# A transformer block on one core: token tile 5 turned on TensorE, values made by head group, loads paced, and odd tiles normalized on GpSimd

## The chip, the cores and the metric

The kernel runs on one core of a Trainium2 chip. A core has five engines, each with its own stream of instructions in a fixed order: TensorE (PE; its weight loads are shown as PEld), VectorE (DVE), ScalarE (ACT), GpSimd (POOL) and SyncE (SP), which here only starts transfers. Sixteen DMA engines move data between HBM and the on-chip memory (SBUF). TensorE writes its results into PSUM, eight banks of 512 fp32 per partition. The metric is device time in microseconds (us) of one execution, as a median over runs.

## The reference, cut to what matters

```python
def _layernorm(x, axis=-1, eps=1e-5):
    m = jnp.mean(x, axis=axis, keepdims=True)
    v = jnp.var(x, axis=axis, keepdims=True)
    return (x - m) / jnp.sqrt(v + eps)

def _A_ref(x, wqkv, wo):          # x: 1 x 2048 x 1024, wqkv: 1024 x 3072, wo: 1024 x 1024
    H = 32; Dh = 32
    qkv = (x @ wqkv).reshape(B, S, 3, H, Dh).transpose(2, 0, 3, 1, 4)
    q, k, v = qkv[0], qkv[1], qkv[2]
    scores = jnp.einsum("bhqd,bhkd->bhqk", q, k) * (Dh ** -0.5)
    p = _softmax(scores, axis=-1)
    o = jnp.einsum("bhqk,bhkd->bhqd", p, v)
    return o.transpose(0, 2, 1, 3).reshape(B, S, D) @ wo

def _B_ref(x, w1, b1, w2, b2):    # w1: 1024 x 3584, w2: 3584 x 1024
    y = _layernorm(x, axis=-1)
    h = _gelu(jnp.einsum("bsd,df->bsf", y, w1) + b1)
    return jnp.einsum("bsf,fd->bsd", h, w2) + b2

xn = _layernorm(x, axis=-1)
out = x + _A_ref(xn, wqkv, wo) * _silu(_B_ref(xn, w1, b1, w2, b2))
```

All inputs are bf16. Every token row of `x` is normalized; the normalized rows feed 32-head attention without a mask and, normalized once more, an MLP. The attention's output is multiplied by the silu of the MLP's output and added to `x`.

## The kernel before, in words

**Tiling.** The 2048 tokens are 16 tiles of 128, the 32 heads 8 head groups of four heads (128 columns of Q, of K and of V). A head group is worked in 8 blocks of 256 queries, a block in 8 units of 256 keys. One unit is 8 score matmuls (L846) into two pairs of PSUM banks and, for each pair, one exponential on ACT over 128 x 1024 scores (L855), which writes a buffer `P`. There are 8 x 8 x 8 units, thus 1024 exponentials. The products P x V (L612) and the sums of the exponentials follow them: DVE adds the buffers up in a tree (L872 and L886, for the first blocks `tree1`, L1209), or PE sums them with a column of ones. All dense work is put between the scores on PE: the projections to Q, K and V of the next head group (`proj`), the MLP, and the product with `wo` at the end. Silu, gelu and most PSUM evacuations are on ACT and DVE.

**Order.** No loop of the kernel issues instructions. Each helper (`dma`, `pool`, `dve`, `act`, `chunk`) adds an operation with its assumed length, a priority and its tokens read and written to `_Plan`. Dense PE work is gathered into items (`_Item`), each a list of matmuls into one PSUM bank with the evacuation behind it, and stands in named queues ("tr", "pro", "q0", "v0", "proj", "mlp", "w2", "wo" among them) with a position, a due time and a `hold`, both counted in score groups. `_Plan.run` plays all engines in assumed time: score matmuls go first on PE, then P x V and the dense items (`pe_step`); the other engines take the ready operation of the lowest priority number (`pick`). What comes out is one fixed order for every engine, and `settle` and `emit` put the semaphore waits into it. A changed length or priority thus moves the order around it too. At run time each engine goes through its order and stands at a wait until it is met; SP is a single queue through which all loads, DMA transposes and stores are started one after the other.

**The start, which the change touches.** Tile t of `x` is loaded into a buffer `xst` (`load_x`, L626). There are ten, all in the memory that is `hT` later; tiles 0 to 9 are issued at the head of SP's queue, with the first head group's weights of K and Q (`load_qk`, `wqk`) behind tile 3, and the weights of V for two head groups (`load_v`, `wv`, 512 KB) behind tile 9. Tiles 10 to 15 reuse buffers, so each of their loads waits for an earlier normalize (`load_x(t, [first[2 * n - 5]])`). For every tile, or for pairs of tiles from tile 4 on:

- DVE takes the statistics with two `bn_stats` (L785), a `bn_aggr` (L788) and an add of eps (L792). Tile 1 is the exception: ACT takes its sums in two passes over 128 x 1024 (`AT = 1`).
- GpSimd raises variance plus eps to the power -0.5 (L794).
- DVE normalizes (`normalize`, L748) into one of four buffers `xnb`, which lie in the memory that is `gw` later.
- Tiles 0 to 3 are turned on PE by eight transposes into one PSUM bank each (`tr_item`) and copied to `xnT` by ACT (L737). Tiles 4 to 15 are turned by DMA transposes that SP starts (L752).

From the turned tiles PE makes Q and K of the first head group in pairs of tiles: `q_item` for the pairs 0 to 2, larger Q pieces behind them, and `k_item` for all eight pairs n = 0 to 7. DVE casts Q to bf16 (L712, L702), ACT casts K (L722). The first scores need pair 0; each further pair of K opens another eighth of the keys. The first three query blocks are worked in an interleaved order while the tiles still come in, and their `P` lie partly in memory that belongs to `w1r`, `w2r`, `V`, `QKT` and `hT` later. V of the first two head groups is made together by eight `v_item`s (16 matmuls of 256 columns each, then one evacuation on DVE, L690) that are held back to the score groups 6 to 13.

When all tiles have been normalized, five GpSimd instructions on 128 x 16 (L818 to L822) work out the factors of the second layernorm, and the MLP can begin.

Of the kernel before, what the change touches and what calls it, by code (L numbers as in the profile page):

```python
# [6 lines left out]
ACT = mybir.ActivationFunctionType  # L7
# [25 lines left out]
class _Plan:  # L33
# [59 lines left out]
    def run(self):  # L93
# [152 lines left out]
        def pe_step(t):  # L246
# [69 lines left out]
            elif v_ok and (mode in "rv" or not d_ok or S["s"] == len(self.s_queue)):  # L316
                use = "v"
            elif d_ok:
                use = "d"
            if use is None:  # L320
# [140 lines left out]
def bass_recurrent_scan__mha_block__mixer_channel_mlp__prompt_kernel(  # L461
# [31 lines left out]
    with ExitStack() as st:  # L493
# [7 lines left out]
        NTR, NWARM, NG0, AT = 4, 8, 3, 1  # L501
# [44 lines left out]
        xst = [h_flat[:, i * 1024:(i + 1) * 1024] for i in range(NXS)]  # L546
        xnb = [gw[:, i * 1024:(i + 1) * 1024] for i in range(4)]
# [72 lines left out]
        XS = lambda t: ("xst", t % NXS)  # L620
# [4 lines left out]
        def load_x(t, extra=()):  # L625
            dma(f"x{t}", lambda e: e.dma_start(xst[t % NXS], x2[t * 128:(t + 1) * 128, :]), 262144, [], [XS(t)],  # L626
# [11 lines left out]
        def load_v(pr):  # L638
            src = A_wqkv[:, 2 * D + pr * 256: 2 * D + (pr + 1) * 256].rearrange("(c p) n -> p c n", p=128)
            dma("wv", lambda e: e.dma_start(wv[:], src), 524288, [], [("wv",)], prio=2, rate=200.0)  # L640
# [5 lines left out]
        for t in range(4, NXS):  # L646
            load_x(t)
        load_v(0)
# [44 lines left out]

        def qk_item(hg, which, tq, wi, pos):
# [21 lines left out]
        def k_item(n):  # L716
            it = _Item("pro", 0.01 * n)
            for dc in range(DC):
                def fn(e, b, dc=dc):
                    return mm(e, bank(b, 0, 256), wqk[wk0][:, dc, :], xnT[:, dc, n * 256:(n + 1) * 256], dc == 0, dc == DC - 1)  # L720
                chunk(it, fn, Q256, [("xnT", 2 * n, dc), ("xnT", 2 * n + 1, dc), ("wqk", wk0)])
# [3 lines left out]

        def tr_item(t):
            it = _Item("pro", t - 10.0)
            it.bank = [2, 3, 4, 5][t]
            tk = ("S", it.bank // 2, it.bank % 2)
# [17 lines left out]
        def normalize(t, rs):  # L747
            first[t] = dve(lambda e: e.tensor_scalar(xnb[t % 4], xst[t % NXS], mv[:, t, 0:1], lnp[:, t, 1:2],  # L748
                                          op0=ALU.subtract, op1=ALU.mult), c_b4(1024) + 118,
                [XS(t), ("mv", t), rs], [("xnb", t % 4)], 1)  # L750
            if t >= NTR:
                dma(f"tr{t}", lambda e: e.dma_start_transpose(xnT[:, :, t * 128:(t + 1) * 128], xnb[t % 4]), 262144,  # L752
                    [("xnb", t % 4)], [("xnT", t, c) for c in range(DC)], prio=0, rate=300.0, occ=1300, lat=1000)
# [10 lines left out]
        for n in range(NPR):  # L764
            groups = [(2 * n,), (2 * n + 1,)] if n < 2 else [(2 * n, 2 * n + 1)]
            for ts in groups:
                if ts == (AT,):
# [698 lines left out]
```

## Time and profile before

The median of three runs is 1036.16 us (1034.75 to 1036.66). One execution was profiled:

| what | value |
|---|---|
| profiled execution, its time | 1036.81 us |
| its span, first to last instruction | 1035.0 us |
| mean granted TensorE clock | 0.997 of full |
| PE busy | 994.5 us, 96% |
| PE weight loads busy | 633.3 us, 61% |
| DVE busy | 955.7 us, 92% |
| ACT busy | 1015.9 us, 98% |
| GpSimd busy | 12.2 us, 1%, 21 instructions |
| ACT's exponentials of 128 x 1024, L855 | 988 of them, 923.6 us |
| DMA moved | 168 MB, 162 GB/s over the span |
| chain that ended last, by engine | ACT 84%, PE 9%, DMA 3%, DVE 2% |

How to read the lines that follow: busy times are sums over instructions, "x24" is a count, and a bracket such as [0.51 <-PE ps L846] says that the engine had stood idle for 0.51 us and that an instruction of line 846 on PE ended this. In a timeline a row begins with the time from the span's start and the length; instructions of one kind that follow each other without a gap share a row with a count, and the length is then that of the whole group. Neighbouring rows can overlap by some 0.1 us: an instruction's row may begin before the row ahead of it has ended. Line numbers are those of the kernel before, and in the profile of the changed kernel those of that kernel, where the same statements stand up to 65 lines lower. The figure behind a DMA group is the median time from issue to landing.

### The profile page before, as it was taken

The numbers are of one execution on the slowest core, as the hardware profiler recorded it, in microseconds if no ns is written. First come the engines' busy times: TensorE is split into PE (matmuls) and PEld (weight loads), VectorE is DVE, ScalarE is ACT, GpSimd is POOL, SyncE is SP. The second block draws the span as 40 slices with busy tenths as digits, with TensorE's granted clock in tenths as the row PEclk, the third lists the DMA queues.
The fourth block names the chain that finished last, engine by engine and source line by source line (L and its number), as shares of the span: only waits on it lengthen the run. The fifth ranks groups of instructions, "written<-read, shape, count | busy, mean of one in ns | idle before, by whom it ended". The sixth has DMA issues, their size and how long they took to land.

```text
span 1035.0 us, 31625 instructions
## 1 busy us (share of the span) xinstructions
PE 994.5 (96%) x14148; PEld 633.3 (61%) x14217; DVE 955.7 (92%) x1343; ACT 1015.9 (98%) x1093; POOL 12.2 (1%) x21
## 2 busy tenths in 40 slices
PE   8999999999999999999999999999999999999996
PEld 6656566666766566666665666666656665654433
DVE  7899999899799999997899999998999889978896
ACT  7999999999999999999999999999999999999996
POOL 2200000000000000000000000000000000000000
PEclk9999999999999999999999999999999999999998
DMA  7967756545766657446457575565365762963321
GB/s 204 171 155 212 192 151 188 166 114 153 205 182 143 177 163 221 120 133 190 136 147 196 149 224 164 149 181 160 84 165 161 208 177 70 294 209 121 121 84 53
DMA packets 318199, 167.99 MB, mean 162 GB/s; under 512 B 56688, under 2 KB 306032, under 8 KB 318064
## 3 DMA queue, kind: packets, MB, share of 16 engines
q1 hardware_dynamic: 318064, 165.98, 58.1%
q8 instruction: 111, 1.82, 0.7%
q14 instruction: 24, 0.20, 0.1%
HBM read 146.55 MB, written 12.06 MB: 153 GB/s over the span
## 4 chain that ended last, share of the span: by engine, by line
ACT 84%; PE 9%; DMA 3%; DVE 2%; issue 0%; SPq 0%; POOL 0%; DVEq 0%; another core or an unknown queue 0%
ACT P L855 78%; PE ps L617 6%; ACT ut L1040 4%; DMA w2r<-in_B_w_dram 2%; PE ps L846 2%; PE ps L612 1%; ACT gw L1067 1%; ACT P L1157 1%; DVE stats L785 1%; DMA xnT<-gw 0%; DMA hT<-in_A_x_dram 0%; DVE gw L748 0%; DVE PA L872 0%; DVE hT L1391 0%; ACT w2r L855 0%
## 5 line engine op out<-in xcount | busy, mean ns | idle before, releaser
L855 ACT ACTIVATE P<-ps 128x1024 bf16<-128x1024 f32 x988 | 923.6, 1238 | 2.9 <-PE ps L846 2.8
L872 DVE TENSOR_TENSOR PA<-P 128x2048 bf16<-128x2048 bf16 x173 | 209.5, 1215 | 33.5 <-ACT P L855 32.4
L617 PE MATMUL ps<-yT,w1r 128*128 128x256 bf16 x1792 | 228.2, 273 | 0.8 <-DVE QKT L702 0.5
L617 PE MATMUL ps<-w2r,hT 128*128 128x256 bf16 x1792 | 223.7, 273 | 4.0 <-DMA w2r<-in_B_w_dram 2.6
L846 PE MATMUL ps<-QKT 32*128 32x256 bf16 x4032 | 200.2, 273 | 12.9 <-ACT P L855 9.3
L886 DVE TENSOR_TENSOR PR<-PR,PA 128x2048 bf16<-128x2048 bf16 x173 | 209.4, 1211 | 1.3
L617 PEld LDWEIGHTS ps<-yT,w1r 128*128 128x128 bf16 x1792 | 163.6, 98 | 54.8 <-issue 30.2
L617 PEld LDWEIGHTS ps<-w2r,hT 128*128 128x128 bf16 x1792 | 163.3, 98 | 54.6 <-issue 30.8
L846 PEld LDWEIGHTS ps<-QKT 32*128 32x128 bf16 x4032 | 59.8, 92 | 142.1 <-ACT P L855 135.3
L612 PE MATMUL ps<-P,V 128*32 128x256 bf16 (+1 forms) x4080 | 136.8, 272 | 0.3 <-issue 0.3
L617 PE MATMUL ps<-xnT,wqk 128*128 128x512 bf16 (+1 forms) x507 | 118.7, 360 | 7.2 <-issue 2.0
L612 PEld LDWEIGHTS ps<-P,V 128*32 128x32 bf16 x4080 | 95.8, 96 | 31.3 <-issue 22.5
L617 PE MATMUL ps<-wv,xnT 128*128 128x256 bf16 (+1 forms) x575 | 85.8, 285 | 0.9 <-DVE QKT L702 0.7
L617 PEld LDWEIGHTS ps<-xnT,wqk 128*128 128x128 bf16 x560 | 49.3, 98 | 53.7 <-issue 15.6
L1023 DVE TENSOR_TENSOR hT<-ps,b1T 128x512 bf16<-128x512 f32 x112 | 76.4, 682 | 1.8 <-PE ps L617 1.1
L872 DVE TENSOR_TENSOR PR<-P 128x2048 bf16<-128x2048 bf16 x60 | 72.6, 1210 | 1.0 <-ACT P L855 0.8
L617 PEld LDWEIGHTS ps<-wv,xnT 128*128 128x128 bf16 x576 | 53.0, 98 | 22.2 <-issue 9.3
L1040 ACT ACTIVATE ut<-ut 128x2048 bf16<-128x2048 bf16 (+1 forms) x33 | 62.1, 1883 | 0.0
L941 DVE STREAM_TRANSPOSE nt<-ps 128x256 f32<-128x256 f32 x63 | 27.8, 442 | 14.9 <-PE ps L612 14.8
L702 DVE CAST QKT<-ps 128x512 bf16<-128x512 f32 x58 | 39.6, 683 | 1.8 <-PE ps L617 1.4
L1037 DVE TENSOR_TENSOR ut<-hT 128x2048 bf16<-128x2048 bf16 (+1 forms) x33 | 34.7, 1052 | 0.1
L1042 DVE TENSOR_TENSOR hT<-ut,hT 128x2048 bf16<-128x2048 bf16 (+1 forms) x33 | 34.6, 1050 | 0.0
(107 smaller groups left out, 581.3 us busy)
## 6 DMA issues: line engine op xcount, KB each, us to landing
w1r<-in_B_w_dram SPq DMA_DIRECT2D x112, 512.0 KB, 4.5
w2r<-in_B_w_dram SPq DMA_DIRECT2D x128, 448.0 KB, 4.6
hT<-in_A_x_dram SPq DMA_DIRECT2D x20, 256.0 KB, 3.8
wqk<-in_A_wqkv_dram SPq DMA_DIRECT2D x16, 256.0 KB, 4.3
yst<-in_A_x_dram SPq DMA_DIRECT2D x16, 256.0 KB, 4.7
g_scratch<-gw SPq DMA_DIRECT2D x32, 128.0 KB, 3.8
o_scratch<-ot SPq DMA_DIRECT2D x56, 64.0 KB, 3.6
xnT<-o_scratch SPq DMA_DIRECT2D x7, 512.0 KB, 7.2
```

The source lines that it names most:

```text
L612: ins = e.matmul(dst(j), lhsT=lhsT(j), rhs=rhs(j), start=start, stop=stop, tile_position=(0, 32 * j), skip_group_check=True)
L617: return e.matmul(dst, lhsT=lhsT, rhs=rhs, start=start, stop=stop, skip_group_check=True)
L702: dve(lambda e: e.tensor_copy(QKT[sl][:, which, tq * 512:(tq + 1) * 512], bank(it.bank)), c_ps(512), [], [(nm, sl, 2 * tq), (nm, sl, 2 * t ...
L846: ins = e.matmul(bank(b0[j], kk * 256, (kk + 1) * 256), lhsT=QKT[sl][32 * j:32 * j + 32, 1, kb * 128:(kb + 1) * 128], rhs=QKT[sl][32 * j:3 ...
L855: x = act(lambda e, h=h: e.activation(Pt[pi][:, 2 * h:2 * h + 2].rearrange("p j k q -> p (j k q)"), ps[:, pr[h] * 1024:(pr[h] + 1) * 1024] ...
L872: return dve(lambda e: e.tensor_tensor(dst[:].rearrange("p u j q -> p (u j) q"), src[:].rearrange("p u j k q -> p (u j) k q")[:, :, 0, :], ...
L886: return dve(lambda e: e.tensor_tensor(fl3(pr), fl3(pr), fl3(PA[i]), op=ALU.add), c_b16(2048), [("PA", i), tok], [tok], 3.2)
L941: dve(lambda e: e.transpose(nt_t[:], bank(pv.bank, 256, 512)), c_ps(256) + 120, [], [("nt",)], prio, pv)
L1023: w1_ev[p] = dve(lambda e: e.tensor_tensor(hT[:, hs], bank(it.bank).rearrange("p (k t) -> p k t", k=2), b1T[:, 2 * pi:2 * pi + 2].unsqueez ...
L1037: dve(lambda e: e.tensor_tensor(u_, x_, x_, op=ALU.mult), c_b16(n), hs_, [("ut", ui)], gp)
L1040: act(lambda e: e.activation(u_, u_, ACT.Tanh, scale=GC), c_acts(n), [("ut", ui)], [("ut", ui)], ga)
L1042: dve(lambda e: e.tensor_tensor(x_, u_, x_, op=ALU.mult), c_b16(n), [("ut", ui)] + hs_, hs_, gp)
```

## The change

The change is made in the start of the kernel and in what feeds it; the rest of the program text is the same, though the planner writes its whole order anew.

1. **Tile 5 on PE** (`TRP = (5,)`). It is turned by PE and copied by ACT like tiles 0 to 3, without a DMA transpose. Its item stands in the queue "pro" just ahead of K of its pair, and `pe_step` lets an item of the queue "tr" in between two matmuls of another item.
2. **Statistics of tile 3 on ACT**, in two passes as for tile 1 (`AT = (1, 3)`).
3. **GpSimd normalizes tiles 7, 9, 11, 13 and 15** (`PN`); DVE keeps the others. The planner assumes 2000 ns for one.
4. **K casts.** For the pairs n = 3 to 7 DVE casts K; ACT keeps n = 0, 1 and 2.
5. **First Q and K in 128 columns.** `qk_first` takes the place of `q_item(0)` and `k_item(0)`: Q and K of tile 0, then those of tile 1 by halves, in 128-column matmuls. K of the pair 1 is split by tile too.
6. **Loads.** There are 16 buffers for tiles of `x`: six more, in the memory of `PR` and `yst`. Tiles 0 to 11 are loaded up front; tiles 12 and 13, the weights of V, and tiles 14 and 15 wait for the normalize of tile 4 (`first[4]`). The loads of the second head group's K weights wait for the normalize of tile 15 instead of tile 9.
7. **V by head group.** `v_half` makes V of one head group for four tiles (32 matmuls of 128 columns, one evacuation). Four of them, for head group 0, stay in the start, held to the score groups 6, 8, 10 and 12; the four of head group 1 become items of the projections that run during head group 0, at the positions 8, 18, 28 and 38.
8. **Smaller ones.** The priority of `tree1` is 2.3 instead of 3.2; the assumed latencies of the DMA transposes of tiles 4, 6 and 7 are longer.

In instructions, the planned PE stream has 14,355 matmuls instead of 14,217, ACT's 1088 activations instead of 1090, DVE's 28 `bn_stats` instead of 30 and 163 tensor copies instead of 158; SP starts 27 DMA transposes instead of 28.

```diff
+            tq, th = self.dense["tr"], heads["tr"]
+            if use is None and S["do"] is not None and th < len(tq) and tq[th].chunks[0].left == 0 and tq[th].chunks[0].ready <= t:
+                heads["tr"] += 1
+                tq[th].k = 1
+                S["mode"] = "d"
+                commit(tq[th].chunks[0], t)
+                return
...
-        NTR, NWARM, NG0, AT = 4, 8, 3, 1
+        TRP = (5,)
+        PN = (7, 9, 11, 13, 15)
+        NTR, NWARM, NG0, AT = 4, 8, 3, (1, 3)
...
+            xst += [pr_flat[:, 0:1024], pr_flat[:, 1024:2048]]
+        xst += [yst_t[i][:] for i in range(2)]
...
-        for t in range(4, NXS):
+        for t in range(NTR, 12):
             load_x(t)
-        load_v(0)
...
+        def v_half(h, m, kind, pos=0.0):
+            it = _Item(kind, pos)
+            for t4 in range(4):
+                for dc in range(DC):
+                    def fn(e, b, t4=t4, dc=dc):
+                        tb = 4 * m + t4
+                        return mm(e, bank(b, t4 * 128, (t4 + 1) * 128), xnT[:, dc, tb * 128:tb * 128 + 128],
+                                  wv[:, dc, h * 128:(h + 1) * 128], dc == 0 and t4 == 0, dc == DC - 1)
+                    chunk(it, fn, Q128, [("xnT", 4 * m + t4, dc), ("wv",)])
+            a = V_SLOTS[0][h]
+            dve(lambda e: e.tensor_copy(V[:, a, 4 * m:4 * m + 4, :], bank(it.bank).rearrange("p (t n) -> p t n", t=4)),
+                c_ps(512), [], [("V", a, 2 * m), ("V", a, 2 * m + 1)], 0, it)
+            return it
...
+            for lo, w in ((0, 128), (128, 128)) if n < 2 else ((0, 256),):
...
+            if n >= 3:
+                dve(lambda e: e.tensor_copy(QKT[0][:, 1, n * 256:(n + 1) * 256], bank(it.bank, 0, 256)), c_ps(256), [],
+                    [("K", 0, n)], -1, it)
+                return it
             act(lambda e: e.activation(QKT[0][:, 1, n * 256:(n + 1) * 256], bank(it.bank, 0, 256), ACT.Copy), c_act(256), [],
                 [("K", 0, n)], -1, it)
...
+        def qk_first():
+            it = _Item("pro", -0.001)
+            for lo, d0, d1 in ((0, 0, 8), (128, 0, 4), (128, 4, 8)):
+                for k, wi in ((0, wq0), (1, wk0)):
+                    for dc in range(d0, d1):
...
+            act(lambda e: e.activation(QKT[0][:, 1, 0:256], bank(1, 0, 256), ACT.Copy), c_act(256), [("S", 0, 1)], [("K", 0, 0)], -1)
+            return it
...
+            rw = ([XS(t), ("mv", t), rs], [("xnb", t % 4)], 1)
+            first[t] = pool(nf, 2000, *rw) if t in PN else dve(nf, c_b4(1024) + 118, *rw)
+            if t >= NTR and t not in TRP:
                 dma(f"tr{t}", lambda e: e.dma_start_transpose(xnT[:, :, t * 128:(t + 1) * 128], xnb[t % 4]), 262144,
...
+            if n == 6:
+                for t in range(12, NT):
+                    load_x(t, [first[4]])
+                    if t == 13:
+                        load_v(0, [first[4]])
...
-                    if t >= NXS:
-                        load_x(t, [first[2 * n - 5]])
...
+            pro_q += [tr_item(t) for t in (2 * n, 2 * n + 1) if t in TRP]
...
-        for n in range(NPR):
-            plan.dense["v0"].append(v_item(0, n, "pro", 0.2 + 0.01 * n))
-            plan.dense["v0"][-1].hold = 6 + 1 * n
+        for n in range(NPR // 2):
+            plan.dense["v0"].append(v_half(0, n, "pro", 0.2 + 0.01 * n))
+            plan.dense["v0"][-1].hold = 6 + 2 * n
...
-            wk = load_qk(hg, 1, [first[9]] if hg == 1 else ())
+            wk = load_qk(hg, 1, [first[NT - 1]] if hg == 1 else ())
...
+            if hg == 1:
+                lst += [(8 + 10 * n, "v1", n) for n in range(NPR // 2)]
```

## The prediction

> **What bounds the kernel now.** I read the busy shares by stretch first, because a mean over the whole span mixes the start with the rest. Columns: busy time (instructions) of PE, PEld, DVE, ACT, POOL, then the granted clock, the DMA share and GB/s.
>
> ```profile
> 0.00:20.00 20.00, 17.34 (x241) 14.95 (x241) 16.11 (x43) 13.69 (x19) 4.40 (x12) 1.00 0.76 213
> 20.00:40.00 20.00, 16.95 (x195) 11.53 (x188) 16.22 (x39) 18.25 (x24) 2.62 (x5) 1.00 0.92 209
> 40.00:60.00 20.00, 18.88 (x360) 13.07 (x359) 18.65 (x31) 19.69 (x24) 5.16 (x6) 1.00 0.95 163
> ...
> 200.00:300.00 100.00, 99.53 (x1414) 66.50 (x1416) 90.90 (x118) 100.00 (x108) 0.00 (x0) 1.00 0.59 161
> ```
>
> From 60 us to 1025 us ACT is the bound: 100.00 of 100 us, and the clock is 1.00, so no throttle is in it. What the change does before 60 us therefore reaches the end one for one, as a shift of ACT's queue, and nothing else counts unless PE, DVE or DMA fall behind ACT later. Second, ACT's own order of time from the first exponential on (start, length, what; in brackets its idle time):
>
> ```profile
> 12.73 1.02 ACT L855 ACTIVATE P<-ps 128x1024 bf16<-128x1024 f32 x1 [0.51 <-PE ps L846]
> 13.65 1.02 ACT L737 ACTIVATE xnT<-ps 128x1024 bf16<-128x1024 bf16 x1
> ...
> 16.70 4.69 ACT L855 ACTIVATE P<-ps 128x1024 bf16<-128x1024 f32 x5 [0.51 <-PE ps L846]
> 22.68 0.38 ACT L722 ACTIVATE QKT<-ps 128x256 bf16<-128x256 f32 x1 [1.28 <-PE ps L617]
> 22.96 4.69 ACT L855 ACTIVATE P<-ps 128x1024 bf16<-128x1024 f32 x5
> ...
> 37.83 1.02 ACT L855 ACTIVATE P<-ps 128x1024 bf16<-128x1024 f32 x1 [0.47 <-PE ps L846]
> ...
> 55.74 1.03 ACT L855 ACTIVATE P<-ps 128x1024 bf16<-128x1024 f32 x1
> ```
>
> Five exponentials take 4.69, so one costs (4.69 - 1.02) / 4 = 0.917. A K cast costs 22.96 - 22.68 = 0.28, and 0.26 at other places: 0.27. Between 12.73 and 55.74 stand 40 exponentials, one transpose copy and seven K casts: 36.7 + 0.9 + 1.9 = 39.5 of 43.0 us. **ACT waits 3.5 us there**, longest before the K cast of tiles 4 and 5. Third, the DMA view of 17 to 21.6 us shows why (engines' busy tenths, then queues, then issue to landing):
>
> ```profile
> DMA  8999999940019999999980097203224755899999
> ...
> q8 instruction: 1, 0.02, 1.4%
> ...
> hT<-in_A_x_dram SPq DMA_DIRECT2D x2, 256.0 KB, 3.7
> xnT<-gw SPq DMA_TRANSPOSE x3, 2.9
> ```
>
> The transpose of tile 5 was issued at 17.09 and released PE at 21.55, after 4.46; the usual one takes 2.9. Beside it ran one instruction fetch, and the engines stood still in the middle. Two more transposes took 6.0 in the stretch 29.8 to 37, again beside one fetch. Fourth, GpSimd, because it gets new work:
>
> ```profile
> 7.96 0.78 POOL L794 TENSOR_TENSOR lnp<-lnp,mhalf 128x1 f32<-128x1 f32 x1 [0.56 <-DVE lnp L792]
> ...
> 40.98 0.23 POOL L818 TENSOR_TENSOR lnp<-lnp 128x16 f32<-128x16 f32 x1
> 41.29 0.29 POOL L819 TENSOR_SCALAR lnp<-lnp 128x16 f32<-128x16 f32 x1
> 41.66 3.04 POOL L820 TENSOR_TENSOR lnp<-lnp,mhalf 128x16 f32<-128x16 f32 x1
> 44.78 0.78 POOL L822 TENSOR_TENSOR lnp<-lnp 128x16 f32<-128x16 f32 x1
> ```
>
> L822 is a multiply of the same size as L818 and took 0.78 against 0.23, while DVE ran two-input adds (L1209); L794 took 0.78 at 7.96, beside a DVE normalize, against 0.55 at 6.85. So a GpSimd instruction waits for some DVE ones. The other way round: inside L820 (41.66 to 44.70) DVE's normalizes took 0.99 for two and its adds 0.68 each, as elsewhere. DVE did not wait.
>
> **The change part by part**, summed on ACT's queue.
>
> *First exponential, +0.5.* Tile 3's statistics move from DVE to ACT (two passes, 1.06 each), and the changed order puts the first of them ahead of the copy of tile 0's transpose. x3 is issued at 2.11 and takes 4.9 to land: 7.0. Then 1.05 of pass, and the copy starts at 8.1 instead of 7.31. Copies of tiles 0, 1, 2 (0.92 each) and the second pass (1.05) end at 11.9; the K cast of tiles 0 and 1 follows, and now tile 3's copy (0.92, from 12.3, when PE has turned it) stands before the first exponential, no longer behind it: 13.25. If x3 takes the median 3.8, PE still sets 12.3: the lower end is +0.5 too; with x3 a microsecond later it is +1.5.
>
> *ACT's work, -1.35.* Five of the seven K casts (tiles 6 to 15) go to DVE: 5 x 0.27. Tile 3's copy leaves the stretch, tile 5's enters it (PE turns it now): even. Left: 36.7 + 0.9 + 0.5 = 38.1.
>
> *ACT's waits, 3.5 to 0.6.* K of tiles 4 and 5 needs the DMA only for tile 4 now: normalize at 14.4, issue 15.0, landing 17.9 (2.9). Q and K of that pair are 16 matmuls of 0.11 and follow two score groups: the cast runs at its turn, about 21.8, without a wait. One hole stays behind it, cast to score matmul to exponential, 0.5 as in the rows above. For the later pairs I walked the changed order with the rows' lengths. The five pows come at 19.1, 21.7, 25.8, 28.7 and 33.1, the transposes land in pairs at 24.2 and 25.5, 26.8 and 28.1, 31.5 and 32.8, 34.2 and 35.5, 37.2 and 39.4. Score groups are 1.83 apart and PE is in order, so a late landing holds the scores queued behind it; spare there is 1.3 us for tiles 4, 6, 7, over 2 for 8 and 9, 0.9 for 10 to 13, 0.3 for 14 and none for 15. Undisturbed, this is -2.9. But the same view has one such fetch in each of 17 to 21.6, 29.8 to 37 and 41.9 to 47.3 us, with transposes of 4.5, 6.0 and 4.3 beside it, 1.4 to 3.1 over the usual. The last six transposes are now in flight from 28 to 39 almost without a break, so I expect one to be hit: +1.0. Two hits: +3.1 (1.7 late each, with the queue behind them). None: 0.
>
> *GpSimd normalize, five of them.* The trace has no such row. From below: IOTA 128x128 took 0.24, MEMSET 128x1 0.10, so about 1.1 ns an element, 1.2 us for 1024, and 0.2 fixed: 1.4. From above: L818's 16 elements in 0.23, 8 ns each, 8 us. I take 1.4, nearest to the row with most elements. In the walk the price is free up to 2.2 us, since each one has the gap to the next pow; 2.6 costs 0.8, 3.0 costs 2.0, 3.5 costs 4.1. [...]
>
> *DVE.* It loses five normalizes (0.45 each), two statistics of 0.6 and an aggregate (1.4), gains five K casts (0.34 each): less work, nothing on the path. The eight V evacuations become four (0.61 each) before 40 us.
>
> *PE.* V of the second head group (64 matmuls of 256 columns, 0.11 each, 7 us) leaves the start and comes back as 128 of 128 columns (eight transposes take 0.45, 0.056 each: 7.2 us) up to unit 78. It lies beside PE's 18.9 of 20 us at 60 to 80 and 19.9 at 80 to 100, under an ACT that is always full; cover gone, it would cost up to 7 there, but ACT showed 100.00 with PE at 99.53. Taken: 0.
>
> *SP.* x10 and x11 are issued before any transpose; x12, x13, V's weights, x14, x15 pass behind tile 4's transpose, 1.5 MB that have landed by 23 at some 350 GB/s, the rate of the loads at 12 to 14 us, just ahead of tile 6's. At worst they hold tile 6's landing by 1.0, inside its spare. The second group's K weights wait for the last normalize: needed at 44, landed by 41.
>
> *Tail.* The chain of waits has 1.21 us of "issue" on PE at 1025.82, in the last rush of small matmuls. The instruction count changes by some 270, so it may vanish (-1.2), stay or grow (+1.2); I take 0.
>
> Sum: +0.5 - 1.35 - 2.9 + 1.0 = **-2.75**. The profiled execution took 1036.81 (span 1035.0 and 1.8 around it): 1034.06. The median of the runs is 0.65 lower, so I forecast 1036.16 - 2.75 = **1033.4**. Its own range is 1032.1 to 1034.1.
>
> **Rivals.** *A, slower: DVE waits for GpSimd.* Both normalizes of a pair are released by the same pow, and if GpSimd's comes first DVE stands for its length, five times, with statistics and casts queued behind; DVE is busy 16.2 of 20 us there, so it does not catch up. Walked so, the last pow moves from 33.1 to 36.1 at 1.4 us each, and the loss is 3.0; at 2.0 us it is 5.5. It turns into a loss from 1.4 us on: 1036.4 there, **1038.9** at 2.0. For it: L822 and L794 show that the two do block each other. Against it: DVE ran through L820 unhindered. The Trainium skill, "SBUF — State Buffer", section "Who interferes with whom", states just this: the shared port pair is an exclusive lock, and whichever of the two starts first fully blocks the other for its whole instruction. By that rule L820 should have held DVE until 44.70; this trace disagrees, though L820 reads only 16 elements.
> *B, no change: two landings late.* 1033.4 + 2.1 = **1035.5**. For it: three of twelve transposes were late before.
> *C, slower: GpSimd's price is 3.5 or more* without any lock: 1033.4 + 4.1 = **1037.5**. For it: only rows of 128 elements and fewer exist.
>
> **How the numbers follow.** The smallest change that these runs tell from none is about 0.2%, 2.07 us. Forecast 0.50, B 0.22, A 0.22, C 0.06. Forecast is faster, B the same, A and C slower: 0.50, 0.22, 0.28. The range goes from 1031.5 (no landing late, and most of the tail's hole gone) to 1039.0 (A at 2.0 us); outside are a longer GpSimd normalize with the lock and a double luck, together under 0.2.
>
> **What would show it.** Right: first exponential at about 13.2; ACT's waits under 2 us between it and the exponential after the six into w2r, and that one at about 52 to 53; two K casts left on ACT there; GpSimd normalizes under 2.2 with DVE's normalizes still near 0.54 and no idle time in front of them. Wrong: DVE idle before its normalizes for as long as GpSimd's run (A); transposes of 10 to 15 taking 4 us or more to land, with scores waiting (B); GpSimd's busy time over 15 us (C); or ACT under 99% busy between 60 and 1000 us, which none of my terms has.

## The result, and the profile after

The changed kernel takes 1038.82 us (median, 1036.30 to 1041.04) where the kernel before takes 1036.33 beside it: 1.0024 times as long, 95% interval 1.0015 to 1.0032. It was forecast to be 2.75 us faster and is 2.5 us slower. One execution was profiled, at 1037.8 us with a span of 1036.0, thus a microsecond under its median.

The busy shares by stretch of the changed kernel, with the columns as before (PE, PEld, DVE, ACT, POOL, granted clock, DMA share, GB/s):

```profile
0.00:20.00 20.00, 16.63 (x244) 14.26 (x245) 15.05 (x44) 16.44 (x24) 4.79 (x12) 1.00 0.75 219
20.00:40.00 20.00, 15.20 (x204) 11.42 (x200) 15.24 (x35) 15.42 (x18) 19.47 (x10) 0.91 0.75 159
40.00:60.00 20.00, 16.95 (x284) 10.75 (x286) 14.01 (x23) 16.95 (x19) 8.29 (x6) 0.91 0.65 125
200.00:300.00 100.00, 99.21 (x1380) 65.29 (x1379) 93.78 (x122) 100.00 (x108) 0.00 (x0) 1.00 0.57 155
```

Up to 20 us ACT has more work done than before (16.44 against 13.69). From 20 to 60 us it has 5.6 us less. GpSimd is busy for 19.47 of 20 us, and the granted clock, 1.00 in the same stretches of the kernel before, is 0.91 in two of them. ACT's order of time:

```profile
13.56 1.02 ACT L911 ACTIVATE P<-ps 128x1024 bf16<-128x1024 f32 x1
...
22.97 3.77 ACT L911 ACTIVATE P<-ps 128x1024 bf16<-128x1024 f32 x4 [0.51 <-PE ps L902]
...
31.56 3.77 ACT L911 ACTIVATE P<-ps 128x1024 bf16<-128x1024 f32 x4 [0.82 <-PE ps L902]
38.36 1.94 ACT L911 ACTIVATE hT<-ps 128x1024 bf16<-128x1024 f32 x2 [3.03 <-PE ps L902]
...
48.68 1.94 ACT L911 ACTIVATE w1r<-ps 128x1024 bf16<-128x1024 f32 x2 [2.58 <-PE ps L902]
...
60.03 15.71 ACT L911 ACTIVATE P<-ps 128x1024 bf16<-128x1024 f32 x17
```

The exponential after the six into w2r, the 41st, comes at 60.03 in place of 55.74: 4.3 us later than in the kernel before, where 52 to 53 was forecast. All waits between the first exponential and this one sum to 7.6 us. Part of the loss comes back later: the waits of 0.71 and 0.64 us that the kernel before has at 176.5 and 917.6 us are not there, and the last of the 1024 exponentials is 2.5 us late. In the tail ACT's wait before its last copy is 2.76 us in place of 4.58, and the span ends 1.0 us late (1036.0 for 1035.0).

GpSimd's order of time has the instruction that the prediction could not see (start, length):

```profile
20.12 3.79 POOL L796 TENSOR_SCALAR gw<-hT,mv,lnp 128x1024 bf16<-128x1024 bf16 x1
23.88 0.72 POOL L846 TENSOR_TENSOR lnp<-lnp,mhalf 128x2 f32<-128x2 f32 x1
24.70 4.05 POOL L796 TENSOR_SCALAR gw<-hT,mv,lnp 128x1024 bf16<-128x1024 bf16 x1
28.73 0.71 POOL L846 TENSOR_TENSOR lnp<-lnp,mhalf 128x2 f32<-128x2 f32 x1
29.54 3.78 POOL L796 TENSOR_SCALAR gw<-PR,mv,lnp 128x1024 bf16<-128x1024 bf16 x1
33.29 0.72 POOL L846 TENSOR_TENSOR lnp<-lnp,mhalf 128x2 f32<-128x2 f32 x1
```

A normalize takes 3.78 to 4.05 us, not 1.4. The pow of the next pair (L846) stands behind it without a gap, so GpSimd goes round in 4.6 to 4.9 us. DVE, in order too, waits for that pow (the view of DVE's waits from 19 to 45 us: total, times, longest):

```profile
DVE gw L796 <- POOL lnp L846: 4.7, 3, 1.8
```

Behind DVE's waiting normalize stand its V evacuations (L716). PE's next V item needs the bank that such an evacuation frees; the scores stand behind the item, and ACT waits for the scores. That is the chain into the 3.03 us. It has one more link, in the clock (the busy shares again, microsecond by microsecond):

```profile
33.00:34.00 1.00, 0.21 (x8) 0.00 (x0) 0.00 (x0) 1.00 (x2) 1.00 (x2) 1.00 0.59 127
34.00:35.00 1.00, 0.00 (x0) 0.00 (x0) 0.96 (x3) 1.00 (x2) 0.90 (x2) 1.00 0.52 120
35.00:36.00 1.00, 0.69 (x10) 0.69 (x11) 1.00 (x3) 0.33 (x1) 1.00 (x1) 0.84 0.71 158
36.00:37.00 1.00, 1.00 (x12) 1.00 (x10) 0.97 (x3) 0.00 (x0) 1.00 (x1) 0.50 1.10 247
```

PE stood nearly still for two microseconds (0.21 us of matmuls from 33 to 35), and then, with its work at hand and ACT idle, it ran at half its clock.

### The profile page after: what moved, and what is told of

It reads as the page before. It is cut to its first block, busy times and chain, and to the rows that moved or that the text cites. A ratio compares the mean times of both kernels' runs of the same rounds, so it can differ in the third digit from the quotient of the medians.

```text
span 1036.0 us, 31979 instructions
## 1 busy us (share of the span) xinstructions
PE 1005.2 (97%) x14355; PEld 638.1 (62%) x14355; DVE 955.5 (92%) x1342; ACT 1017.0 (98%) x1093; POOL 32.6 (3%) x26
## 4 chain that ended last, share of the span: by engine, by line
ACT 90%; PE 4%; DVE 2%; POOL 2%; issue 1%; DMA 1%; SPq 0%; DVEq 0%
ACT P L911 82%; ACT ut L1101 4%; PE ps L630 3%; POOL gw L796 1%; ACT gw L1128 1%; ACT P L1221 1%; PE ps L625 1%; DVE stats L837 1%; PE ps L902 1%; ACT w2r L911 1%; POOL lnp L846 0%; DMA hT<-in_A_x_dram 0%; ACT w1r L911 0%; DMA xnT<-gw 0%; DVE gw L796 0%
## 5 line engine op out<-in xcount | busy, mean ns | idle before, releaser
L630 PE MATMUL ps<-xnT,wqk 128*128 128x512 bf16 (+2 forms) x584 | 131.5, 356 | 1.7 <-DMA xnT<-gw 0.6
L630 PE MATMUL ps<-wv,xnT 128*128 128x256 bf16 (+2 forms) x704 | 90.3, 268 | 6.2 <-DVE V L716 3.0
L630 PEld LDWEIGHTS ps<-wv,xnT 128*128 128x128 bf16 x704 | 56.8, 100 | 30.3 <-issue 11.4
```

The lines of the kernel that those rows point to most:

```text
L630: return e.matmul(dst, lhsT=lhsT, rhs=rhs, start=start, stop=stop, skip_group_check=True)
```

## The experiments

The runs are compared by the ratio of their time to that of the kernel before, measured beside them (its medians there were 1035.5 to 1036.3):

| kernel | median us | ratio to before, 95% |
|---|---|---|
| changed | 1038.82 | 1.0024 (1.0015 to 1.0032) |
| before_gp | 1042.23 | 1.0057 (1.0045 to 1.0068) |
| gp512 | 1037.15 | 1.0010 (1.0000 to 1.0019) |
| gp256 | 1036.67 | 1.0003 (0.9995 to 1.0012) |
| gp256_late_yx | 1033.05 | 0.9973 (0.9962 to 0.9983) |
| all_dve | 1032.38 | 0.9966 (0.9954 to 0.9978) |
| all_dve_k_act | 1034.66 | 0.9983 (0.9972 to 0.9995) |
| all_dve_x_late | 1034.48 | 0.9990 (0.9980 to 0.9999) |
| all_dve_v_pairs | 1033.55 | 0.9982 (0.9973 to 0.9990) |
| all_dve_tr5_dma | 1039.80 | 1.0035 (1.0023 to 1.0047) |
| all_dve_wv_late | 1030.95 | 0.9950 (0.9937 to 0.9962) |
| plan_3900 | 1036.42 | 1.0006 (0.9998 to 1.0015) |

The first theory was *price*: the GpSimd normalize is too long. Its rivals were *order* (something else in the new order costs the time) and *lock* (GpSimd and DVE hold each other up, and the row is long only for that).

### Only the GpSimd instruction shorter: gp256 and gp512

```diff
+            w_ = 256 if t in PN else 1024
             def nf(e):
-                return e.tensor_scalar(xnb[t % 4], xst[t], mv[:, t, 0:1], lnp[:, t, 1:2], op0=ALU.subtract, op1=ALU.mult)
+                return e.tensor_scalar(xnb[t % 4][:, 0:w_], xst[t][:, 0:w_], mv[:, t, 0:1], lnp[:, t, 1:2],
+                                       op0=ALU.subtract, op1=ALU.mult)
```

The planner's assumed length stays, so all engines keep the changed kernel's order. In gp512, w_ is 512. The other columns of these five tiles are left out.

> The changed kernel in its own order, but GpSimd normalizes only the first 256 of the 1024 columns of tiles 7, 9, 11, 13 and 15; the other columns of these tiles are left out (they keep an earlier tile's values). Theory price: in the changed kernel such an instruction took 3.79 to 4.05 us and the next pair's pow stood behind it, so that GpSimd went 4.8 us a pair; with a quarter of the columns it takes about 1.1 us, DVE no longer stands before its normalizes (1.27 to 1.77 us each now), and the exponential after the six into w2r comes at 52 to 53 us in place of 60.0; the time is 1032.5 to 1035. Theory order (the new order, the V halves or the paced loads cost the time, not the instruction): GpSimd's rows shrink, but that exponential stays at 57 us or later and the time at 1037 or more.

> As the run with 256 columns, with 512 of 1024 columns normalized by GpSimd and the others left out. Theory price: about 2.0 to 2.1 us an instruction, which the prediction put just under the free limit of 2.2, so within 1 us of the run with 256 columns and 3 to 5 us ahead of the changed kernel. If the loss grows in step with the length instead, it lies a third of the way from the 256-column run to the changed kernel. Theory order: no difference to the changed kernel, 1038 to 1039.

The normalize took 1.22 to 1.49 us with 256 columns and 2.08 to 2.35 with 512. The times are 1036.67 and 1037.15: 2.1 and 1.4 thousandths under the changed kernel, and 0.5 us from each other. So the length counts. That it costs nothing up to some 2.3 us, as the prediction's walk had it (free up to 2.2), shows in the pows of the later pairs: they come at 25.75, 29.89 and 34.20 in gp256 and at 25.71, 29.98 and 34.26 in gp512. The equal totals would not show it alone, since both kernels were then held at one later place, by tile 15's transpose. But neither kernel came down to 1033.4. ACT's order of time in gp256 shows that place:

```profile
34.81 1.95 ACT L913 ACTIVATE hT<-ps 128x1024 bf16<-128x1024 f32 x2
36.62 3.81 ACT L913 ACTIVATE P<-ps 128x1024 bf16<-128x1024 f32 x4
40.23 2.03 ACT L913 ACTIVATE hT<-ps 128x1024 bf16<-128x1024 f32 x2
45.58 1.94 ACT L913 ACTIVATE w1r<-ps 128x1024 bf16<-128x1024 f32 x2 [3.31 <-PE ps L904]
```

Up to the 25th exponential (38.43 in gp256, 39.91 in the kernel before) it was 1.5 us ahead of the kernel before. Then ACT waited 3.31 us at one place, for scores that stood behind the transpose of the last tile. SP's order of time there:

```profile
35.52 1.23 SPq L802 DMA_TRANSPOSE xnT<-gw  x1
36.80 0.58 SPq L1068 DMA_DIRECT2D yst<-in_A_x_dram  x1
37.42 1.24 SPq L802 DMA_TRANSPOSE xnT<-gw  x1
```

The transpose of tile 14 took 2.7 us to land. That of tile 15, issued at 37.42, took 5.4: it landed at 42.83, 1.56 us behind the load into yst (41.27) that went out just ahead of it. In the kernel before, both loads into yst went out at 34.19 and 35.73, ahead of tile 12's transpose. Two edits of the change move them: its x tiles 14 and 15 now lie in the buffers yst, and the loads' own condition, which was tile 11's normalize, is taken out:

```diff
-                    [("yst", t2)], rate=390.0, extra=[first[11]] if c == 0 else [w1_ev[4]] if c == 1 else ())
+                    [("yst", t2)], rate=390.0, extra=[w1_ev[4]] if c == 1 else ())
```

So the first of these loads waits for tile 14's normalize to free its buffer, and falls between the last two transposes. *Order* was right too, at a place of its own.

### The two loads into yst behind the last transpose: gp256_late_yx

```diff
-                    [("yst", t2)], rate=390.0, extra=[w1_ev[4]] if c == 1 else ())
+                    [("yst", t2)], rate=390.0, extra=[first[NT - 1]] if c == 0 else [w1_ev[4]] if c == 1 else ())
```

> The run with 256 columns on GpSimd (the other columns left out), and the first two loads into yst wait for tile 15's normalize, as they are then issued behind its transpose. In the 256-column run that transpose was issued at 37.42, right behind one of these loads, and landed at 42.83, 1.56 us after the load; ACT waited 3.31 us for it. Theory load ahead (a transpose lands only after the loads issued before it): the transpose takes 2.7 to 3.2 us, that wait is under 1 us, the exponential after the six into w2r comes near 53.5 in place of 56.90, and the time is 1032.5 to 1034.5, as the prediction had it for a short GpSimd instruction. Theory instruction fetch (what made it late ran beside it): it stays at 4.5 us or more and the time at 1036 to 1037.

1033.05 us, and the 41st exponential came at 53.99, as *load ahead* had it. But tile 15's transpose still took 4.5 us to land, as *instruction fetch* had it: a fetch ran from 39.07 to 40.1 beside it, and one from 39.16 to 40.3 in gp256. The load's part was about 1 us (5.4 to 4.5). The transpose landed 1.5 us earlier (41.35), the clock, halved in gp256 from 42.75 on, stayed at 1.00, and the wait shrank to 0.71:

```profile
42.94 5.74 ACT L913 ACTIVATE w1r<-ps 128x1024 bf16<-128x1024 f32 x6 [0.71 <-PE ps L904]
48.56 5.61 ACT L913 ACTIVATE w2r<-ps 128x1024 bf16<-128x1024 f32 x6
53.99 13.02 ACT L913 ACTIVATE P<-ps 128x1024 bf16<-128x1024 f32 x14
```

With a GpSimd normalize of the predicted length and this load out of the way, the change gives 1033.05 where 1033.4 was forecast. ACT's waits up to the 41st exponential come to 1.8 us there, for 0.6 and 1.0 in the sum.

### The change without its GpSimd part, and the GpSimd part alone: all_dve and before_gp

```diff
-        PN = (7, 9, 11, 13, 15)
+        PN = ()
```

> The change without its GpSimd part: DVE normalizes all tiles, everything else as in the changed kernel (the planner's order shifts a little around it). Theory price: DVE pays 5 x 0.45 us more, which fits into its idle time between 20 and 45 us; 1033 to 1035.5, ahead of both kernels. Theory order: 1037 or more, as the other parts cost the time.

In before_gp the kernel before gets the other half:

```diff
-            first[t] = dve(lambda e: e.tensor_scalar(xnb[t % 4], xst[t % NXS], mv[:, t, 0:1], lnp[:, t, 1:2],
-                                          op0=ALU.subtract, op1=ALU.mult), c_b4(1024) + 118,
-                [XS(t), ("mv", t), rs], [("xnb", t % 4)], 1)
+            def nf(e):
+                return e.tensor_scalar(xnb[t % 4], xst[t % NXS], mv[:, t, 0:1], lnp[:, t, 1:2], op0=ALU.subtract, op1=ALU.mult)
+            rw = ([XS(t), ("mv", t), rs], [("xnb", t % 4)], 1)
+            first[t] = pool(nf, 2000, *rw) if t in (7, 9, 11, 13, 15) else dve(nf, c_b4(1024) + 118, *rw)
```

> The kernel before with one part of the change alone: GpSimd normalizes tiles 7, 9, 11, 13 and 15. Theory price: about 3.9 us each, the pows of the pairs 8 to 11 and the last normalize come 2 to 4 us later than before; slower than before by 2 to 4.5 us, 1038.5 to 1041. Theory order: the instruction alone does no harm, 1035.5 to 1037.5. Theory lock (GpSimd and DVE hold each other up, by DVE's share of work): DVE's rows beside a GpSimd normalize are longer by about a microsecond each.

all_dve takes 1032.38 us, 0.34% under the kernel before; before_gp takes 1042.23, 0.57% over it and more than expected. One part of the change costs about 6 us in either kernel, and the others together gain 3.5. In before_gp's trace the clock stays at 1.00 until the tail (0.50 only from 1034.94 on), and yet ACT's waits up to the 41st exponential come to 6.9 us. So GpSimd's round can cost this much without the clock.

In all_dve the two last tiles are normalized in one go, and both transposes go out ahead of the yst loads. One large wait is left in its start:

```profile
22.44 3.77 ACT L911 ACTIVATE P<-ps 128x1024 bf16<-128x1024 f32 x4 [0.50 <-PE ps L902]
27.88 1.94 ACT L911 ACTIVATE V<-ps 128x1024 bf16<-128x1024 f32 x2 [1.66 <-PE ps L902]
```

PE had waited for V's weights there (landed at 24.44), and its V matmuls then ran at a granted clock of 0.50 from 24.58 to 28.0: 25 of them took 2.79 us, where the same 25 take 1.57 at 1.00 in all_dve_x_late below. Tile 6's transpose, at 26.74, came late as well. But in the traces of all_dve_k_act and all_dve_v_pairs it lands as late (26.76 and 26.77) while the clock stays at 1.00, and ACT waits only 0.41 and 0.86 us there. So half or more of the 1.66 goes with the halved clock, and this execution (1033.48) was the longest of all_dve's five.

### The GpSimd normalize by itself: price

A small kernel repeats one instruction of each kind, three in a row:

```diff
+            (lambda e: pn(e, 1024), None),
+            (p_small, None),
+            (None, d_alone),
+            (lambda e: pn(e, 1024), d_stats),
+            (lambda e: pn(e, 1024), d_norm),
+            (lambda e: pn(e, 1024), d_add),
+            (lambda e: pn(e, 1024), d_cast),
+            (p_mul, None),
+            (p_copy, None),
```

> A small kernel that computes nothing of the reference (it copies x to the output) and runs the GpSimd normalize by itself: 128 x 1024, 512, 256 and 128 columns with DVE idle, then 128 x 1024 beside a stream of DVE statistics, of DVE normalizes, of DVE two-input adds and of DVE casts from PSUM, and a one-operation multiply and a plain copy. Theory price: about 3.8 us for 1024 columns with DVE idle, 3.4 ns an element (from 1.22, 2.08 and 3.79 us for 256, 512 and 1024 columns in the runs so far), and at most 0.3 us more beside any DVE stream. Theory lock: about 1.4 us alone, and 3 us or more only beside DVE streams; or DVE instructions that stand for the length of a GpSimd one.

GpSimd's order of time. The first four rows are normalizes of 1024 columns beside DVE statistics, DVE normalizes, DVE adds and DVE casts; then the multiply alone and the copy:

```profile
32.76 11.31 POOL L31 TENSOR_SCALAR po<-xa,sc 128x1024 bf16<-128x1024 bf16 x3 [8.00 <-DVE do L74]
45.94 11.90 POOL L31 TENSOR_SCALAR po<-xa,sc 128x1024 bf16<-128x1024 bf16 x3 [1.87 <-DVE ds L55]
63.69 15.42 POOL L31 TENSOR_SCALAR po<-xa,sc 128x1024 bf16<-128x1024 bf16 x3 [5.85 <-DVE do L31]
79.57 11.31 POOL L31 TENSOR_SCALAR po<-xa,sc 128x1024 bf16<-128x1024 bf16 x3 [0.46 <-DVE do L60]
90.98 8.49 POOL L40 TENSOR_SCALAR po<-xa,sc 128x1024 bf16<-128x1024 bf16 x3
99.54 3.00 POOL L45 COPY po<-xa 128x1024 bf16<-128x1024 bf16 x3
```

A normalize takes 3.77 us (11.31 / 3) beside statistics and casts, and 2.08, 1.22 and 0.80 for 512, 256 and 128 columns with DVE idle: some 0.4 us and 3.3 ns an element a partition. With one operation in place of two it takes 2.83, a copy 1.00. So *price* holds for what the kernel does, and *lock* as the cause falls. A part of it is there: beside DVE normalizes it takes 3.97, and DVE's go at about 0.75 each for 0.48 alone (16 in 12.0 us against 4 in 1.92); beside two-input adds it takes 5.14, outside what *price* had expected.

The Trainium skill, "GPSIMD Engine Reference", section 3.1, gives 1.03 cycles an element for bodies of up to two operations and calls about 1.8, at 1.2 GHz, the best case of a tight loop; an estimate from these two figures is 0.9 to 1.5 us for 1024 elements. That is far below the measured 3.77, and the measurement decides. The Trainium skill's advice in the same section, to use DVE for elementwise work, is what these runs come to. By the Trainium skill, "SBUF — State Buffer", section "Who interferes with whom", the ports that the two share are an exclusive lock: where a DVE instruction needs them too, the one that starts first fully blocks the other. That is not what ran here: both went on, at 0.75 for 0.48 and 3.97 for 3.77.

### The planner told the true price: plan_3900

```diff
-            first[t] = pool(nf, 2000, *rw) if t in PN else dve(nf, c_b4(1024) + 118, *rw)
+            first[t] = pool(nf, 3900, *rw) if t in PN else dve(nf, c_b4(1024) + 118, *rw)
```

> The changed kernel with one number changed: its planner assumes 3900 ns for a GpSimd normalize in place of 2000, about what it takes, and writes its order by that. In the changed kernel PE stood at half its clock twice, from 35.68 to 39.09 and from 45.92 to 49.34, each time after a stretch of 3.41 us with at most 1.3 us of PE work; matmuls that ACT waited for took 1.15 and 1.4 us longer by it. Theory clock: the order now has warm-up matmuls in the stalls it knows of, the clock stays at 1.00, and the time falls by 1 to 2.5 us, to 1036.3 to 1037.8. Theory pace: GpSimd's 4.8 us a pair sets the end whatever the order, 1038 to 1040.

1036.42 us, 2.4 under the changed kernel, with the same instructions. The time is where *clock* had it, but not by warm-up matmuls, of which no more were put in (115 in both). The order changed: GpSimd takes one pow ahead of a normalize, which lets DVE go on.

```profile
28.25 0.71 POOL L846 TENSOR_TENSOR lnp<-lnp,mhalf 128x2 f32<-128x2 f32 x1
29.30 1.00 POOL L846 TENSOR_TENSOR lnp<-lnp,mhalf 128x2 f32<-128x2 f32 x1 [0.34 <-DVE lnp L844]
29.99 3.94 POOL L796 TENSOR_SCALAR gw<-PR,mv,lnp 128x1024 bf16<-128x1024 bf16 x1
```

The clock still fell once, from 46.42 to 49.83. How much of the changed kernel's loss is the clock and how much GpSimd's round was not separated by a run of that kernel. An estimate from the matmuls that ACT waited for, at half and at full clock, is 1.15 us for the first halved stretch and 1.2 for the second; the expectation above has 1.4 for the second, but the 25 matmuls of this wait took 2.04 us for about 1.09 and the scores 0.61 for 0.40.

### The prediction's other terms: all_dve_k_act, all_dve_tr5_dma, all_dve_v_pairs

All three start from all_dve. K casts on ACT again:

```diff
-            if n >= 3:
+            if n >= NPR:
```

> The change without GpSimd normalizes, and with all K casts on ACT again. The prediction's term: five casts of 0.27 on the bound engine, 1.35 us slower than the run with all normalizes on DVE: 1033.4 to 1034.1. If ACT's waits in the start swallow them: no difference, 1032.0 to 1032.8.

0.17 points slower than all_dve, some 1.8 us, where the term was 1.35; the two intervals overlap, so the size is not settled. Tile 5 by DMA:

```diff
-        TRP = (5,)
+        TRP = ()
```

> The change without GpSimd normalizes, and with tile 5 turned by DMA as before. Theory of the prediction: the wait of 1.28 us for tile 5 comes back, and the copy of 0.92 us leaves ACT: 0.3 to 1.5 us slower than with tile 5 on PE, 1032.7 to 1033.9. Rival: the DMA transpose lands in time behind tile 4's, since the loads are paced now, and the kernel gains the copy: 1031.3 to 1031.9.

7 us slower than all_dve, outside both expectations. The second transpose stands in SP's queue ahead of all five paced loads, tile 15's load lands at 27.31 in place of 25.76, tile 6's transpose at 28.14 and tile 7's at 31.20 in place of 27.63. Then the clock is halved for 6.83 us from 32.49 on. ACT's order of time:

```profile
23.01 0.38 ACT L754 ACTIVATE QKT<-ps 128x256 bf16<-128x256 f32 x1 [1.83 <-PE ps L630]
...
35.46 1.94 ACT L911 ACTIVATE P<-ps 128x1024 bf16<-128x1024 f32 x2 [4.13 <-PE ps L902]
```

So tile 5 on PE is worth more than its own wait: the 1.28 us of the kernel before come back as 1.83, and the queue behind it pays the rest. V in pairs of head groups:

```diff
-        for n in range(NPR // 2):
-            plan.dense["v0"].append(v_half(0, n, "pro", 0.2 + 0.01 * n))
-            plan.dense["v0"][-1].hold = 6 + 2 * n
+        for n in range(NPR):
+            plan.dense["v0"].append(v_item(0, n, "pro", 0.2 + 0.01 * n))
+            plan.dense["v0"][-1].hold = 6 + 1 * n
...
-            if hg == 1:
+            if hg == -1:
```

> The change without GpSimd normalizes, and with V of both head groups made in the start as before (8 items of 16 matmuls of 256 columns). The prediction costed this part at nothing, since PE's work lay beside a full ACT. Theory hidden: within 0.7 us of the run without it, 1031.7 to 1033.1. Theory PE full: 7 us of matmuls more between 25 and 58 us, where PE is busy for 7.3 to 9.8 of 10 us; 2 to 5 us slower, 1034.5 to 1037.5.

1033.55 us, 0.16 points over all_dve, between the two expectations; the intervals overlap, so the size is not settled. Up to the 41st exponential, at 53.10, it lost nothing. From there to the 60th it took 20.1 us against 18.5 in all_dve. PE came late with the P x V products, and ACT waited twice (2.18 and 0.37):

```profile
59.09 5.61 ACT L911 ACTIVATE P<-ps 128x1024 bf16<-128x1024 f32 x6 [2.18 <-PE ps L625]
```

Just ahead of this PE was not full but stood, for a DVE evacuation of V (L702) that had DVE adds before it:

```profile
56.64 0.28 PE L630 MATMUL ps<-xnT,wqk 128*128 128x256 bf16 x1 [1.86 <-DVE V L702]
```

### Loads out of the transposes' way: all_dve_x_late and all_dve_wv_late

Tiles 14 and 15 later:

```diff
-                    load_x(t, [first[4]])
+                    load_x(t, [first[4] if t < 14 else first[8]])
```

> The change without GpSimd normalizes, and tiles 14 and 15 are loaded after tile 8's normalize in place of tile 4's. In the run without this, tile 6's transpose was issued at 20.44 and landed at 26.74, 0.98 us after the load of tile 15; ACT waited 1.66 us before the exponential at 27.88. Theory load ahead: that transpose lands by 25 us, the 1.66 us go, and if nothing else comes late the time is 1030.5 to 1031.7. Rival: the statistics of tiles 14 and 15 come late instead, their transposes land 2 us later, and the time is 1032 to 1034.

The wait at 27.88 went (tile 6's transpose landed at 25.37), but the time is 1034.48, and the rival as it was worded did not come. Tile 10's transpose, with the loads of 26.9 ahead of it, landed at 33.85 against 33.97 in all_dve, and those of tiles 14 and 15 at 41.32 and 43.80 against 42.53 and 43.46. The loss came later: PE had 0.98 us of work between 38.20 and 41.61, the clock was halved for the 6.83 us behind that, and ACT waited 1.15 us at 45.27 and 1.28 at 48.49. The 41st exponential came at 55.79, in all_dve at 53.76. The wait at 27.88 had been put down to tile 6 before these two runs; with V's matmuls at full clock in all_dve_x_late, the run does not separate the two. The weights of V later, with tiles 12 to 15 where they were:

```diff
                 for t in range(12, NT):
                     load_x(t, [first[4]])
-                    if t == 13:
-                        load_v(0, [first[4]])
+                load_v(0, [first[8]])
...
-            plan.dense["v0"][-1].hold = 6 + 2 * n
+            plan.dense["v0"][-1].hold = 8 + 2 * n
```

> The change without GpSimd normalizes; tiles 12 to 15 are loaded after tile 4's normalize and the weights of V after tile 8's, so that 1.0 MB and not 1.5 MB stands ahead of tile 6's transpose; the V items are held to the score groups 8, 10, 12 and 14. Theory load ahead: tile 6's transpose lands at 24 to 25 in place of 26.74, the wait of 1.66 us at 27.88 is gone, 1030.5 to 1032. Rival clock: PE has less to do from 22 to 29 us without V, one stretch of 3.41 us falls under 1.6 us of work, the clock halves, and the time is 1032.5 to 1034.

1030.95 us, 0.50% under the kernel before and 0.74 points under the changed one: the lowest ratio of all, though its interval overlaps that of all_dve (its five times, 1030.79 to 1031.05, all lie under all_dve's, 1032.20 to 1033.48). Tile 6's transpose landed at 24.53, the 41st exponential came at 51.38, and the clock stayed at 1.00. The planner also put in more warm-up matmuls by itself (88 in place of 50 between 16 and 50 us), so the moved load and the fuller PE came together, and no run separates them. All of ACT's waits from 12.8 to 60 us in this kernel (total, times, longest):

```profile
ACT P L910 <- PE ps L901: 0.5, 1, 0.5
ACT xnT L784 <- PE ps L780: 0.3, 1, 0.3
```

## Why the prediction was wrong, point by point

**GpSimd normalize: wrong, and it decided.** The step that failed is the choice within its bounds. The measured 3.77 to 4.05 us lies between them, 1.4 and 8; the value taken was the lower one, "nearest to the row with most elements", and with it the term was put at nothing ("free up to 2.2 us"). That row was an IOTA of 128 elements, which has more elements than the other rows but no arithmetic on an input: a copy of 1024 elements costs 1.00 and two operations on it 3.77. At this length GpSimd's round of 4.6 to 4.9 us delays the pow that DVE waits for; gp256, gp512, all_dve and before_gp, which change that instruction's length or its engine, and price, which measures it alone, show this from four sides. Rival C (3.5 us or more) was the case that came, with 0.06 of the chance. The walk under it came near: at 2.1 per half microsecond beyond 3.0, it gives some 5.8 us at 3.9 and 1039.2, against the measured 1038.82. That is partly luck, since the walk has no halved clock in it.

**SP: wrong by an omission.** The prediction counted the loads of x and of weights, but not the two loads into yst, whose condition the diff exchanges. In the changed kernel the slow GpSimd hides this, as tile 15's transpose goes out 2.2 us behind that load and lands in 2.9 us. With a short normalize it costs 3.0 thousandths (gp256 against gp256_late_yx). So the forecast gain would not have come even with a normalize of 1.4 us: gp256, at 1.22 to 1.49, is at 1.0003. The last of the paced loads, "landed by 23", landed at 25.46, and tile 6's transpose 0.97 behind them, at 26.43, where 24.2 was forecast.

**ACT's waits, 3.5 to 0.6, plus 1.0 for one late landing: wrong in the changed kernel (7.6), right without GpSimd and with the loads sorted out** (0.5 in all_dve_wv_late). That transposes beside an instruction fetch are late was read rightly, and more traces bear it out (4.3 us against 2.8, below). That a load issued ahead goes with the same was in the same rows of the kernel before, and was not seen.

**The clock: missing.** "No throttle is in it" was read off the kernel before and taken for granted after. In these traces the fall follows PE's own gaps: every fall to half speed between 12 us and the tail came behind a stretch of 3.41 us in which PE had at most 1.61 us of work (below). So a wait of 2 us on PE can bring half speed behind it, and the prediction had no term for that.

**Rival A: not the cause.** GpSimd and DVE do slow each other (in the changed kernel a DVE normalize took 1.18 and 1.09 us beside a running GpSimd one, and 0.55 otherwise), and DVE did stand before its normalizes, as A's sign said. But it stood for the pow queued behind GpSimd's own normalize, not for a port.

**Right, as far as shown.** The first exponential came at 13.56 for 13.25 (12.86 to 13.66 over the kernels that have this start). Two K casts are left on ACT in the stretch. The casts' 1.35 has the right sign (some 1.8 in all_dve_k_act); its size is not settled. DVE's busy time from 20 to 60 us fell, as forecast (15.24 and 14.01 of 20 us, before 16.22 and 18.65), though its order then stood behind GpSimd's pow. V by head group costs nothing where it went, as costed: ACT is full in the changed kernel from 60 to 200 us. What it may gain near 59 us (1.6 in the two traces) was not counted. The tail was taken at 0, within 1.2 either way; it came 1.5 us shorter, so its sign was open and its size outside.

## What to carry to other kernels

Price an instruction by a row that does the same arithmetic on as many elements; if there is none, the price is a range, and the forecast has to be the side of the range on which the sum turns. On an in-order queue look at every transfer whose condition the diff exchanges, not only at those it adds: it moves to another place in the queue, and may stand ahead of something that matters more. And count a stall of two microseconds on PE as more than its length, since in these traces PE's work of the next 3.4 us could run at half its clock.

## What the runs showed that I had not expected

**The clock falls by stretches of 3.41 us, and PE need not be idle in all of it.** In every profile of the whole kernel the changes of the granted clock lie on a grid of 3.41 us, whose start differs between executions. After 12 us and before the tail, eight stretches at full clock held only 0.40 to 1.61 us of matmuls, in seven of the kernels, and each was followed by one at 0.50; every one with 1.65 us or more kept 1.00. Back to 1.00 it came only behind a stretch that was nearly full (3.28 us or more); 2.43 and 2.69 us did not do. So a stall of some 2 us can cost nothing, or half of the next 3.41 us, by where the grid lies. The ends of matmuls are modelled in a trace, so the edge between 1.61 and 1.65 is not sharp. all_dve_wv_late, none of whose stretches has under 2.3 us of work, spread over 0.26 us in five executions, the changed kernel over 4.7 in sixteen; that the grid is the reason is argued from this, not shown. The Trainium skill, "TensorE: Matmul & The Clock Gate", section "What's actually happening", has the half rate and the window of about 3.4 us, and the trace agrees; where it speaks of an idle window, the runs here differ: windows with 1.61 us of work, 47% of them, were followed by half rate, and one with 1.65, 48%, was not.

**Two things go with a late DMA transpose, and they add up.** These are all DMA transposes of the first 60 us in the traces of the kernel before, the changed one and the experiments (171 of them), from issue to landing, by whether an instruction fetch was in flight at any time in between, and whether a plain load issued ahead landed more than 1.7 us after the transpose's issue. With neither, the median is 2.83 us (83 of them, 3.50 at most); with a fetch alone 4.32 (41); with such a load alone 4.50 (16); with both 5.79 (31). For the load a run moved the cause: without it in gp256_late_yx, tile 15's transpose fell from 5.4 to 4.5. For the fetch the cause is argued, not shown, since no run moved a fetch alone, and a transpose that takes long has more chance to meet one. Behind the paced loads (tiles 12 to 15 and V's weights, or some of them) tile 6's transpose lands 0.83 to 1.00 us after the last of them in these traces: 0.97 in the changed kernel (26.43 behind 25.46), 0.98 in all_dve (26.74, 25.76), 0.99 in all_dve_wv_late (24.53, 23.54), 0.83 in all_dve_tr5_dma (28.14, 27.31). Elsewhere it can be more: 1.56 us for tile 15 in gp256.
